# First pairs loaded four tokens to a partition, and attention values multiplied in 64x64 quarters, in a fused attention and feed-forward kernel

## The chip, the cores and the metric

The kernel runs on one core of one Trainium2 chip. A core has a matrix engine (TensorE, PE in the profile, with its weight loads as PEld), VectorE (DVE), ScalarE (ACT) and GpSimd (POOL), which run their own instruction streams and wait for each other by semaphores, and a queue of transfers that SyncE (SP) issues. On-chip memory is SBUF, 128 partitions wide, and PSUM, where TensorE's products land[...]. The metric is device time in microseconds; the time before is the median of three runs.

## The reference

Two blocks follow each other, all in fp32:

```python
# q, k, v: (8, 12, 448, 64)
q_n, k_n = rmsnorm(q, g_q), rmsnorm(k, g_k)          # x / sqrt(mean(x*x) + 1e-6) * g
scores = (1 / sqrt(64)) * q_n @ k_n.transpose(0, 1, 3, 2)
attn = softmax(scores)                                # over the keys
x = (attn @ v) as (8*448, 12*64)                      # 3584 tokens, 768 wide
h = x @ w_in                                          # w_in (768, 1024)
solu = h * softmax(h)
out = layernorm(solu) * g_ln @ w_out                  # w_out (1024, 768)
```

The weights arrive as 64-bit floats, so the kernel converts them itself.

## The kernel before

Only `fast_path` matters here (a general path stands behind a branch for unusual inputs). It has three stages: attention, the product with `w_in` (line 990), the product with `w_out` (line 1205). The last two use a scheme with seven products of sub-blocks instead of eight, and this change doesn't touch them.

Attention runs over 24 *quads* m = 0 to 23. A quad is four heads in two pairs, a = 2m and b = 2m + 1. 448 tokens are three blocks of 128 keys (kc = 0, 1, 2) and a last block of 64. Each fp32 product that the program writes appears as two TensorE instructions in the profile. Per quad:

- `scores(n, kc)` (line 812) makes the scores of one pair and key block: keys on the output's partitions, 448 queries on its columns, in four 64x64 tiles of the array (two halves of the keys by two heads), into a PSUM tile `s` of two banks. `exponentials` (line 802, ScalarE) turns `s` into `E`. `scores_last(m)` (line 825) does the last 64 keys of both pairs. So a quad has seven score units, and seven exponentials.
- `values_last(m)` (line 858) starts the output tiles `o` of both pairs with the last key block, in 64x64 tiles.
- `values(n)` (line 869) adds the three big key blocks of pair n: 128 keys on the array's rows and a head's 64 columns, so two tiles of 128x64, one per head.
- `sums(m)` (line 891) sums `E` over the keys with a matrix of ones, in tiles of 128x32, partly after `add` (line 839, VectorE) and `add_more` (line 848, GpSimd) have added some of the `E` tiles. `inverse` (lines 902 to 910) and `divide` (lines 917, 918) follow on VectorE and GpSimd, and `store_x` (line 926) writes the result to DRAM.

For later quads the same loop body prepares q and k: `squares` (672, ScalarE) and `row_sums` (680, VectorE) for quad m + 2, `fold_sums` (690, 691, GpSimd), `rsqrt_seed` (697, 698, ScalarE) and `rsqrt_step` (704 to 707, VectorE), `normalise` (713, GpSimd), `qk_transpose` (723, VectorE, in 32x32 blocks) and `gain` (727, ScalarE, scales the transposed q) for quad m + 1.

The order is written out by hand (`tc.manual_schedule()`): each engine gets its instructions in the order in which the program names them, and the tile framework adds the semaphore waits that the data require. `unit(f)` names one step of TensorE work and then what is due by `later`. PSUM tiles `s` and the sums tile `sm` share a ring of three buffers (tag "t"), the two `o` tiles another of two.

In twelve quads (`steps_at`: m = 4 to 10, 12, 14, 16, 18, 20) `begin(m)` issues two ScalarE instructions that convert part of `w_in`: line 535, and line 536, which reads what line 535 wrote. `step` issues the VectorE rest (541, 542) a quad later. They stand between the first and the second pair's values in the program.

Pairs 0 and 1 (quad 0) take another way, for a quick start: `load_rows` (line 738) loads tokens to partitions, 112 partitions by four tokens, from SP's and ScalarE's queues; `square_rows` (748, 750), `sum_rows` (756), `normalise_rows` (772, in place), `transpose_rows` (778, TensorE, four transposes of 112 columns into one PSUM tile) and `take_rows` (784 to 788) give the transposed q and k. `gain_column` makes the per-feature gain from `g_q` and `g_k`. Before that, `warm_up` (766) keeps TensorE busy with a product of zeros.

The lines of the loop body that order ScalarE around the values are, before the change:

```python
            if next2:
                squares(a + 4)
                squares(b + 4)
                row_sums(a + 4)
            if next1:
                gain(a + 2)
                gain(b + 2)
            ...
            unit(outputs)        # values_last(m), values(a)
            step(m - 2)
            begin(m)             # lines 535, 536 in twelve quads
            step(m - 1)
            ...
            unit(lambda: values(b))
            unit(lambda: sums(m))
```

Of the kernel before, what the change touches and what calls it, by code (L numbers as in the profile page):

```python
# [9 lines left out]
FP32 = mybir.dt.float32  # L10
U32 = mybir.dt.uint32
I32 = mybir.dt.int32
AX = mybir.AxisListType.X
AF = mybir.ActivationFunctionType
OP = AluOpType
# [351 lines left out]
def fast_path(  # L367
# [24 lines left out]
    nc = tc.nc  # L392
    B, H, S, D = q.shape
    DM, DFF = moe_w_in.shape
    P = 128
# [336 lines left out]
    def load_rows(n, queues):  # L732
        b, hp = divmod(n, NP)
        d = st[n] = {}
        d["qk"] = xs.tile([P, 2, 4, P], FP32, tag="x", name="x")[0:R]
        for s, src in enumerate((q, k)):
            for h in range(2):
                queues[2 * s + h].dma_start(
                    d["qk"][:, s, :, h * D : (h + 1) * D], src[b, 4 * (hp // 2) + hp % 2 + 2 * h].rearrange("(j p) d -> p j d", p=R)
                )  # L740

    def square_rows(n, s, engine):
        d = st[n]
        if s == 0:
            d["sq"] = xs.tile([P, 2, 4, P], FP32, tag="x", name="xsq")[0:R]
        x, y = d["qk"][:, s], d["sq"][:, s]
        if engine is nc.scalar:
            nc.scalar.activation(y, x, AF.Square)
        else:
            engine.tensor_tensor(y, x, x, OP.mult)  # L750

    def sum_rows(n, s):
        d = st[n]
        if s == 0:
            d["ss"] = small.tile([P, 4 * NB], FP32, tag="ss", name="ss", bufs=2)[0:R, 0:16]
        nc.vector.tensor_reduce(
            d["ss"][:, s * 8 : s * 8 + 8], d["sq"][:, s].rearrange("p j (h d) -> p (j h) d", h=2), AX, OP.add
        )

    def warm_up():  # L760
# [4 lines left out]
        for _ in range(5):  # L765
            nc.tensor.matmul(o, w[:, 0:P], w, start=True, stop=True)

    def normalise_rows(n, s):
        d = st[n]
        x = d["qk"][:, s].rearrange("p j (h d) -> p (j h) d", h=2)  # L770
        y = d["y"][:, s * 8 : s * 8 + 8].rearrange("p i -> p i ()").to_broadcast([R, 8, D])
        nc.vector.tensor_tensor(x, x, y, OP.mult)

    def transpose_rows(n, s):
        d = st[n]
        d["pt", s] = ps_t.tile([P, S], FP32, tag="o", name="pt", bufs=2)
        for j in range(4):
            nc.tensor.transpose(d["pt", s][:, j * R : (j + 1) * R], d["qk"][:, s, j], ident[0:R, 0:R])

    def take_rows(n, s):  # L780
        d = st[n]
# [22 lines left out]
    def scores(n, kc):  # L804
        d = st[n]
        s = ps_t.tile([P, 2, 512], FP32, tag="t", name="s")

        for c in range(0, P, D):
            for h in range(2):
                hh = slice(h * D, (h + 1) * D)  # L810
                keys = slice(NJ * c + kc, NJ * (c + D - 1) + kc + 1, NJ)
                nc.tensor.matmul(  # L812
                    s[c : c + D, h, 0:S], d["qkT"][hh, 1, keys], d["qkT"][hh, 0, :],
                    start=True, stop=True,
                )
        exponentials(d, kc, s)
# [19 lines left out]
    def add(n):  # L836
        d = st[n]
        d["es"] = work.tile([P, 2, S], FP32, tag="es", name="es")
        nc.vector.tensor_tensor(d["es"], d["E", 0], d["E", 1], OP.add)  # L839

    def whole(n):
        return on_vector(n // 2) or n % 2 == 0

# [6 lines left out]
    def values_last(m):  # L850

        d = quads[m]
        for i in range(2):
            o = st[2 * m + i]["o"] = ps_t.tile([P, S], FP32, tag="o", name="o", bufs=2)
        for h in range(2):
            for i in range(2):
                pp = slice(i * D, (i + 1) * D)
                nc.tensor.matmul(  # L858
                    st[2 * m + i]["o"][h * D : (h + 1) * D, :], d["vl"][pp, h], d["E", NJ][pp, h],
                    start=True, stop=False,  # L860
                )

    def values(n):


        d = st[n]
        for kc in range(NJ):
            for h in range(2):
                nc.tensor.matmul(  # L869
                    d["o"][h * D : (h + 1) * D, :], quads[n // 2]["v"][:, n % 2 + 2 * h, kc], d["E", kc][:, h],  # L870
                    start=False, stop=(kc == NJ - 1),
                )
# [444 lines left out]
    def unit(f, steps=4):  # L1317
        nonlocal now
        f()
        now += steps  # L1320
        due = [x for x in todo if x[0] <= now]
        todo[:] = [x for x in todo if x[0] > now]
        for _, g in sorted(due, key=lambda x: x[0]):
            g()
# [40 lines left out]
    with tc.manual_schedule():  # L1365
# [19 lines left out]
        for m in range(NQ):  # L1385
            a, b = 2 * m, 2 * m + 1

            def outputs():
                values_last(m)
                values(a)  # L1390


            next1 = m + 1 < NQ
            next2 = m + 2 < NQ
            next3 = m + 3 < NQ
            early = m > 0 and next1

            def norms_next():
                rsqrt_seed(norms[m + 1])
                rsqrt_step(norms[m + 1])  # L1400
                normalise(a + 2)
                normalise(b + 2)

            if m == 0:
                unit(lambda: scores(a, 0))
                normalise_rows(1, 0)
                normalise_rows(1, 1)
                unit(lambda: scores(a, 1))
                unit(lambda: scores(a, 2))
                squares_half(3, 0, True)  # L1410
                for s in range(2):
                    transpose_rows(1, s)
                    take_rows(1, s)
                squares(2)
                squares_half(3, 1, False)
                add(a)
                add_more(a)
                row_sums(2)
                unit(lambda: scores_last(m))
                row_sums(3)  # L1420
                fold_sums(1)
                unit(lambda: scores(b, 0))
                unit(lambda: scores(b, 1))
                add(b)
                norms_next()
                unit(lambda: scores(b, 2))
                squares(4)
                row_sums(4)
                squares(5)
                unit(outputs)  # L1430
                qk_transpose(2)
                gain(2)
                row_sums(5)
                qk_transpose(3)
                fold_sums(2)
                unit(lambda: values(b))
                unit(lambda: sums(m))
                inverse(m)
                later(1, lambda m=m: divide(m))
                continue  # L1440
            if early:
                norms_next()
            for x in joins_at.get(m, ()):
                combine_in(x)
            if next1:
                load_v(m + 1)
            if m == 1:
                load(m + 3)
            unit(lambda: scores(a, 0))
            if m == 1:  # L1450
                gain(3)
            store_x(m - 1)
            if early:
                qk_transpose(a + 2)
                if next3 and m > 1:
                    load(m + 3)
            unit(lambda: scores(a, 1))
            unit(lambda: scores(a, 2))
            unit(lambda: scores_last(m))
            unit(lambda: scores(b, 0))  # L1460
            unit(lambda: scores(b, 1))
            if early:
                qk_transpose(b + 2)
            add(a)
            if not on_vector(m):
                add_more(a)
            unit(lambda: scores(b, 2))
            if next2:
                squares(a + 4)
                squares(b + 4)  # L1470
                row_sums(a + 4)
            if next1:
                gain(a + 2)
                gain(b + 2)
            if next2:
                row_sums(b + 4)
                fold_sums(m + 2)
            add(b)
            if on_vector(m):
                add_more(a)  # L1480
                add_more(b)
            unit(outputs)
            step(m - 2)
            begin(m)
            step(m - 1)
            if m - 1 in sets:
                load_next()
            if m == 2:
                load_next()
                load_next()  # L1490
            if m == 3:
                norm_gain()
            unit(lambda: values(b))
            if m == NQ - 1:
                block_sums(0, 0)
                block_sums(0, 1)
                load_x(1)
            unit(lambda: sums(m))
            inverse(m)
            if next1:  # L1500
                later(1, lambda m=m: divide(m))
            if m == NQ - 2:
                load_x(0)
                sizes(0)
# [188 lines left out]
```

## Time and profile before

| what | value |
|---|---|
| median of three runs (lowest, highest) | 802.53 us (802.07, 803.22) |
| the profiled execution's time | 803.36 us |
| its span, first to last instruction | 801.6 us |
| mean granted TensorE clock | 0.999 |
| first score product starts | 10.58 us |
| attention's last sums end, `w_in` product starts | 316.26 us |
| one quad of attention, from 33 us to 296 us | 12.52 us (12.83 for m = 3) |
| TensorE / VectorE / ScalarE / GpSimd busy | 98% / 77% / 59% / 65% |

A line of the order of time gives start and length in us, the engine, the kernel's line, the operation, output and inputs by the program's names, the tile of the array (rows*columns) for TensorE, the shape and how many instructions were merged into the line. A bracket holds idle time before it and what ended that. TensorE's instructions overlap, so the distance from start to start says more than the lengths. In a line of waits stand the engine and line that waited, what it waited for, the total in us, how often, and the longest. ACTq is the sequencer of ScalarE, which runs semaphore-only instructions.

### The profile page before, as it was taken

The page shows a single profiled execution, that of the slowest core. Times are in us where ns is not written, and L with a number is a line of the kernel's source. Part 1 is how long each engine was busy: PE and PEld are TensorE (multiplying, and loading weights), DVE is VectorE, ACT ScalarE, POOL GpSimd, SP SyncE. Part 2 cuts the span into 40 slices and gives each one's busy share as a digit, 9 for nine tenths or more (in the row PEclk, how much of TensorE's full clock was granted, in tenths as well). Part 3 has the DMA queues.
Part 4 walks back from the last instruction along what each step waited for, and adds up shares of the span by engine and source line. Part 5 has one row for each costly group of instructions (what it writes and reads, how often), then busy time and mean ns, then how long its engine had stood idle before and what let it go on. Part 6 is the DMA issues. An engine that isn't in the chain of part 4 may idle for free.

```text
span 801.6 us, 14271 instructions
## 1 busy us (share of the span) xinstructions
PE 788.1 (98%) x4854; PEld 462.7 (58%) x4854; DVE 613.7 (77%) x1202; ACT 472.2 (59%) x783; POOL 523.1 (65%) x664
## 2 busy tenths in 40 slices
PE   8999999999999999999999999999999999999997
PEld 4344444444444443444444444444789999999996
DVE  6787989989888896488878666777896776866945
ACT  6677878878778774376766544444515455464420
POOL 2666777778876784234456467668698777877861
PEclk9999999999999999999999999999999999999999
DMA  9878889897787832445554435552757457366312
GB/s 169 164 174 156 175 194 186 194 189 161 169 157 169 158 102 75 136 117 155 152 146 131 113 98 141 142 137 52 190 167 233 147 183 264 123 221 223 112 61 83
DMA packets 269598, 122.68 MB, mean 153 GB/s; under 512 B 187596, under 2 KB 254668, under 8 KB 269516
## 3 DMA queue, kind: packets, MB, share of 16 engines
q1 hardware_dynamic: 254332, 111.78, 55.9%
q10 hardware_dynamic: 15184, 9.90, 4.5%
q8 instruction: 40, 0.66, 0.3%
q14 instruction: 42, 0.34, 0.1%
HBM read 84.94 MB, written 36.70 MB: 152 GB/s over the span
## 4 chain that ended last, share of the span: by engine, by line
PE 87%; DVE 3%; DMA 2%; SPq 2%; POOL 2%; ACT 2%; issue 1%; DVEq 0%; ACTq 0%; POOLq 0%
PE A L1205 14%; PE A L990 13%; PE o L869 12%; PE s L812 12%; PE B L990 8%; PE B L1205 7%; PE C L990 4%; PE sm L891 4%; PE D L990 4%; PE C L1205 3%; PE s L825 2%; PE o L858 2%; SPq L636 1%; DMA xg<-xd 1%; ACT E L802 1%
## 5 line engine op out<-in xcount | busy, mean ns | idle before, releaser
L802 ACT ACTIVATE E<-s 128x896 f32<-128x896 f32 x168 | 138.8, 937 | 8.3 <-PE s L812 7.8
L812 PE MATMUL s<-qkT 64*64 64x448 f32 x1152 | 120.1, 545 | 1.0 <-ACT qkT L786 0.6
L869 PE MATMUL o<-E,v 128*64 128x448 f32 x576 | 113.8, 543 | 0.0
L1079 POOL TENSOR_TENSOR he<-he,mhalf 128x1 f32<-128x1 f32 x28 | 27.4, 977 | 102.5 <-DVE he L1078 97.4
L812 PEld LDWEIGHTS s<-qkT 64*64 64x64 f32 x1152 | 48.0, 163 | 59.4 <-ACT E L802 29.3
L1205 PE MATMUL A<-w_out,sums 128*128 128x192 f32 x392 | 79.9, 327 | 1.6 <-POOL sums L1185 1.2
L869 PEld LDWEIGHTS o<-E,v 128*64 128x64 f32 x576 | 39.1, 137 | 72.2 <-issue 68.0
L1205 PE MATMUL B<-w_out,sums 128*128 128x192 f32 x392 | 79.8, 326 | 0.5 <-DVE P L1267 0.5
L713 POOL TENSOR_TENSOR qkn<-qk,ny 128x896 f32<-128x896 f32 x46 | 77.2, 1699 | 3.8 <-DMA qk<-in_q_dram 1.5
L848 POOL TENSOR_TENSOR es<-es,E 128x896 f32<-128x896 f32 x22 | 46.4, 2110 | 48.8 <-ACT sq L672 34.0
L990 PE MATMUL B<-w_in,xsum 128*128 128x512 f32 x168 | 76.7, 592 | 0.0
L990 PE MATMUL A<-w_in,xg 128*128 128x512 f32 x168 | 74.6, 593 | 0.0
L1061 ACT ACTIVATE u<-h,hmax 128x1024 f32<-128x1024 f32 x28 | 32.2, 1148 | 66.8 <-DVE hmax L1055 66.8
L1205 PEld LDWEIGHTS A<-w_out,sums 128*128 128x128 f32 x392 | 66.1, 190 | 2.4 <-POOL sums L1185 1.5
L1205 PEld LDWEIGHTS B<-w_out,sums 128*128 128x128 f32 x392 | 66.2, 190 | 0.8 <-DVE P L1267 0.8
L839 DVE TENSOR_TENSOR es<-E 128x896 f32<-128x896 f32 x48 | 53.9, 1124 | 2.7 <-ACT E L802 2.7
L990 PEld LDWEIGHTS B<-w_in,xsum 128*128 128x128 f32 x168 | 31.9, 190 | 40.2 <-issue 39.2
L990 PEld LDWEIGHTS A<-w_in,xg 128*128 128x128 f32 x168 | 31.8, 190 | 40.1 <-issue 39.3
L690 POOL COPY ss<-part 32x56 f32<-32x56 f32 x92 | 47.0, 511 | 5.9 <-DVE part L680 1.4
L680 DVE TENSOR_REDUCE part<-sq 128x28 f32<-128x896 f32 x46 | 47.9, 1080 | 3.9 <-ACT sq L672 1.6
L723 DVE STREAM_TRANSPOSE qkT<-qkn 128x896 f32<-128x896 f32 x46 | 48.4, 1087 | 0.0
L563 POOL TENSOR_TENSOR w_out<-w_out 128x384 f32<-128x384 f32 x44 | 45.0, 1028 | 1.3
(153 smaller groups left out, 1651.0 us busy)
## 6 DMA issues: line engine op xcount, KB each, us to landing
ur<-ud SPq DMA_DIRECT2D x60, 256.0 KB, 4.6
ud<-ub SPq DMA_DIRECT2D x112, 128.0 KB, 2.3
xd<-xo SPq DMA_DIRECT2D x48, 224.0 KB, 3.0
qk<-in_q_dram SPq DMA_DIRECT2D x92, 112.0 KB, 3.1
qk<-in_k_dram SPq DMA_DIRECT2D x92, 112.0 KB, 3.0
v<-in_v_dram SPq DMA_DIRECT2D x24, 384.0 KB, 4.3
out_dram<-P SPq DMA_DIRECT2D x19, 384.0 KB, 4.2
raw<-in_moe_w_in_dram SPq DMA_DIRECT2D x12, 512.0 KB, 5.3
```

The source lines that it names most:

```text
L563: nc.gpsimd.tensor_tensor(o, p, q, OP.subtract)
L680: nc.vector.tensor_reduce(norms[m]["part"][:, i], st[n]["sq"], AX, OP.add)
L690: e.tensor_copy(ss[g * 32 : g * 32 + 32], part[o * 32 : o * 32 + 32])
L713: e.tensor_tensor(d["qkn"].rearrange("p (s b) d -> p s b d", s=2), d["qk"].rearrange("p s (b d) -> p s b d", d=32), y.rearrange("p (s b) - ...
L723: nc.vector.transpose(d["qkT"].rearrange("p s t -> p (s t)"), d["qkn"].rearrange("p b d -> p (b d)"))
L802: nc.scalar.activation(d["E", kc], s[:, :, 0:S], AF.Exp)
L812: nc.tensor.matmul(s[c : c + D, h, 0:S], d["qkT"][hh, 1, keys], d["qkT"][hh, 0, :], start=True, stop=True,)
L839: nc.vector.tensor_tensor(d["es"], d["E", 0], d["E", 1], OP.add)
L848: e.tensor_tensor(d["es"], d["es"], d["E", 2], OP.add)
L869: nc.tensor.matmul(d["o"][h * D : (h + 1) * D, :], quads[n // 2]["v"][:, n % 2 + 2 * h, kc], d["E", kc][:, h], start=False, stop=(kc == NJ ...
L990: nc.tensor.matmul(k[bank], a[:, c], w_in[i][:, c], start=begin and c == 0, stop=c == HD - 1, skip_group_check=not begin,)
L1205: nc.tensor.matmul(k[bank], a[:, c].rearrange("p a i -> p (a i)"), w_out[:, area, i, c], start=begin and c == 0, stop=c == KC - 1, skip_gr ...
```

## The change

Four things change.

1. First pairs. `load_rows` puts four successive tokens on a partition, (p j) in place of (j p), so that a partition's run in DRAM is 1 KB instead of 256 B. `normalise_rows` writes into the tile of the squares instead of in place, in the order that the transposes want; transpose j writes every fourth column of the PSUM tile, so that tokens come out in order.
2. Values of quads 1 to 22 (`halved`). `values_part(m, part)` replaces `values(a)` and `values(b)`: both pairs at once, in 64x64 tiles, half of each key block's rows a time. In part 0 pair a uses rows 0 to 63 and pair b rows 64 to 127; in part 1 they change over, so each row tile writes into the other pair's PSUM bank.
3. Between the parts stands `turn(m)`: an empty ScalarE instruction that waits for the last product of part 0, and for which the first product of part 1 waits. On ScalarE it is named after `begin(m)`.
4. Order. The score unit (a, 0) of the next quad is named between the two parts, so its exponential comes before the next quad's seeds; a quad m > 1 starts with unit (a, 1). `gain(a + 2)` goes ahead of the squares, `gain(b + 2)` behind `turn`.

VectorE, GpSimd and SP keep the order of their instructions.

```diff
@@ load_rows
-        d["qk"] = xs.tile([P, 2, 4, P], FP32, tag="x", name="x")[0:R]
+        d["qk"] = xs.tile([P, 2, 2, 4, D], FP32, tag="x", name="x")[0:R]
...
-                    d["qk"][:, s, :, h * D : (h + 1) * D], src[b, 4 * (hp // 2) + hp % 2 + 2 * h].rearrange("(j p) d -> p j d", p=R)
+                    d["qk"][:, s, h], src[b, 4 * (hp // 2) + hp % 2 + 2 * h].rearrange("(p j) d -> p j d", p=R)
@@ normalise_rows, transpose_rows
-        x = d["qk"][:, s].rearrange("p j (h d) -> p (j h) d", h=2)
-        y = d["y"][:, s * 8 : s * 8 + 8].rearrange("p i -> p i ()").to_broadcast([R, 8, D])
-        nc.vector.tensor_tensor(x, x, y, OP.mult)
+        y = d["y"][:, s * 8 : s * 8 + 8].rearrange("p (h j) -> p h j ()", h=2).to_broadcast([R, 2, 4, D])
+        o = flat(d["sq"][:, s]).rearrange("p (j h d) -> p h j d", h=2, d=D)
+        nc.vector.tensor_tensor(o, d["qk"][:, s], y, OP.mult)
...
-            nc.tensor.transpose(d["pt", s][:, j * R : (j + 1) * R], d["qk"][:, s, j], ident[0:R, 0:R])
+            nc.tensor.transpose(
+                d["pt", s].rearrange("p (r j) -> p j r", j=4)[:, j], flat(d["sq"][:, s])[:, j * P : (j + 1) * P], ident[0:R, 0:R]
+            )
@@ new
+    def halved(m):
+        return 0 < m < NQ - 1
...
+    def values_part(m, part):
+        first = None
+        for kc in range(NJ):
+            for i in range(2):
+                d = st[2 * m + i]
+                pp = slice((part ^ i) * D, (part ^ i) * D + D)
+                for h in range(2):
+                    x = nc.tensor.matmul(
+                        d["o"][h * D : (h + 1) * D, :], quads[m]["v"][pp, i + 2 * h, kc], d["E", kc][pp, h],
+                        start=False, stop=(part == 1 and kc == NJ - 1),
+                    )
+                    first = first or x
+        if part == 0:
+            quads[m]["half"] = x
+        else:
+            behind(first, quads[m]["turn"])
...
+    def turn(m):
+        x = quads[m]["turn"] = nc.scalar.nop()
+        behind(x, quads[m]["half"])
@@ loop over quads
                 values_last(m)
-                values(a)
+                if halved(m):
+                    values_part(m, 0)
+                else:
+                    values(a)
...
-            unit(lambda: scores(a, 0))
             if m == 1:
+                unit(lambda: scores(a, 0))
                 gain(3)
+            else:
+                unit(lambda: scores(a, 1))
             store_x(m - 1)
...
-            unit(lambda: scores(a, 1))
+            if m == 1:
+                unit(lambda: scores(a, 1))
             unit(lambda: scores(a, 2))
...
             unit(lambda: scores(b, 2))
+            if next1:
+                gain(a + 2)
             if next2:
                 squares(a + 4)
                 squares(b + 4)
                 row_sums(a + 4)
-            if next1:
-                gain(a + 2)
-                gain(b + 2)
...
-            unit(lambda: values(b))
+            if halved(m):
+                turn(m)
+                gain(b + 2)
+                unit(lambda: scores(a + 2, 0))
+                unit(lambda: values_part(m, 1))
+            else:
+                unit(lambda: values(b))
```

More of the change, by code (lines that the diff above doesn't have):

```diff
@@ L744, in square_rows @@
         if s == 0:
-            d["sq"] = xs.tile([P, 2, 4, P], FP32, tag="x", name="xsq")[0:R]
+            d["sq"] = xs.tile([P, 2, 2, 4, D], FP32, tag="x", name="xsq")[0:R]
         x, y = d["qk"][:, s], d["sq"][:, s]
@@ L756, in sum_rows @@
         nc.vector.tensor_reduce(
-            d["ss"][:, s * 8 : s * 8 + 8], d["sq"][:, s].rearrange("p j (h d) -> p (j h) d", h=2), AX, OP.add
+            d["ss"][:, s * 8 : s * 8 + 8], d["sq"][:, s].rearrange("p h j d -> p (h j) d"), AX, OP.add
         )
@@ L766, in warm_up, with flat @@
             nc.tensor.matmul(o, w[:, 0:P], w, start=True, stop=True)
+    def flat(x):
+        return x.rearrange("p h j d -> p (h j d)")
     def normalise_rows(n, s):
         d = st[n]
-        x = d["qk"][:, s].rearrange("p j (h d) -> p (j h) d", h=2)
-        y = d["y"][:, s * 8 : s * 8 + 8].rearrange("p i -> p i ()").to_broadcast([R, 8, D])
-        nc.vector.tensor_tensor(x, x, y, OP.mult)
+        y = d["y"][:, s * 8 : s * 8 + 8].rearrange("p (h j) -> p h j ()", h=2).to_broadcast([R, 2, 4, D])
+        o = flat(d["sq"][:, s]).rearrange("p (j h d) -> p h j d", h=2, d=D)
+        nc.vector.tensor_tensor(o, d["qk"][:, s], y, OP.mult)
     def transpose_rows(n, s):
@@ L861, in values_last, with behind @@
                 )
+    def values_part(m, part):
[14 more added lines that the diff above has]
+            behind(first, quads[m]["turn"])
+    def behind(x, y):
+        tc.add_manual_dep(
+            getattr(x, "ins", x), getattr(y, "ins", y).name,
+            mybir.DependencyInfo(mybir.DependencyClass.Sync, mybir.DependencyReason.DATA),
+            reason="row tiles change banks",
+        )
+    def turn(m):
+        x = quads[m]["turn"] = nc.scalar.nop()
+        behind(x, quads[m]["half"])
     def values(n):
```

## The prediction

> **What bounds the kernel now.** I read the page's head first, then TensorE's order of time over one quad of heads, then ScalarE's over the same quad.
>
> ```profile
> span 801.6 us, 14271 instructions
> PE 788.1 (98%) x4854; PEld 462.7 (58%) x4854; DVE 613.7 (77%) x1202; ACT 472.2 (59%) x783; POOL 523.1 (65%) x664
> PEclk9999999999999999999999999999999999999999
> ```
>
> TensorE is busy for 98% of the span at the full clock, so a microsecond that is added to or taken from its stream counts in full. In attention the stream repeats every 12.52 us (145.55 to 158.07 below; columns: start, length, engine, line, what):
>
> ```profile
> 145.55 0.93 PE L858 MATMUL o<-E,vl 64*64 64x448 f32 x8
> 146.41 4.73 PE L869 MATMUL o<-E,v 128*64 128x448 f32 x24
> 151.07 0.96 PE L891 MATMUL sm<-E,ones 128*32 128x224 f32 x16
> 151.85 0.94 PE L891 MATMUL sm<-es,ones 128*32 128x224 f32 x16
> 152.72 2.52 PE L812 MATMUL s<-qkT 64*64 64x448 f32 x24
> 155.06 0.93 PE L825 MATMUL s<-qkT 64*64 64x448 f32 x8
> 155.81 2.44 PE L812 MATMUL s<-qkT 64*64 64x448 f32 x24
> 158.07 0.93 PE L858 MATMUL o<-E,vl 64*64 64x448 f32 x8
> ```
>
> From start to start, 24 score instructions in 64x64 quarters (four at a time, 6 steps) take 158.07-155.81 = 2.26 us, 0.376 a step. The last-block values (8 instructions, 2 steps, 0.75 us of work) take 0.86: 0.11 is lost where the array goes from 64x64 to 128x64. The main values (24, two at a time, 12 steps, 4.51 us of work) take 4.66. Their first step takes 0.43 (the weight loads stand at 146.41, 146.84, 147.21), 0.05 over; the remaining 0.10 goes at the change to 128x32.
>
> ScalarE in that quad:
>
> ```profile
> 141.29 5.77 ACT L802 ACTIVATE E<-s 128x896 f32<-128x896 f32 x7
> 146.88 1.84 ACT L672 ACTIVATE sq<-qk 128x896 f32<-128x896 f32 x2
> 148.57 1.27 ACT L727 ACTIVATE qkT<-qkT,gcol 128x448 f32<-128x448 f32 x2
> 149.69 0.82 ACT L535 ACTIVATE tmp<-raw,seven 128x512 f32<-128x512 uint32 x1
> 150.54 0.63 ACT L536 ACTIVATE tmp<-tmp 128x512 int32<-128x512 f32 x1
> ```
>
> It has time to spare per quad, but its order matters below. From these starts: an exponential every 0.80 (5.59/7), a square every 0.84, a gain every 0.56, and L536 0.85 after L535. L535 and L536 convert input weights; the pair stands in 12 of the 24 quads (m = 4 to 10, 12, 14, 16, 18, 20), always before TensorE's sums.
>
> **What the Trainium skill says.** "TensorEngine Tiling (Array Packing)", Key Properties: a change of tiling mode drains the array. The 0.11 and 0.10 agree. Same page, Gotcha 1: different row tiles may not use one PSUM bank at the same time and software has to order them; that is why the change has a wait between the two halves of the values. "Perfetto Trace Analysis", DVE / Act Engine Instruction: an instruction is pushed into a wait queue, and then the sequencer is free for the next one. The trace differs, in the only place where it matters here. Two consecutive ScalarE lines, and the semaphore-only instruction that follows them in the program (L1085's, in the first feed-forward product):
>
> ```profile
> 435.74 0.63 ACT L535 ACTIVATE tmp<-raw,seven 128x384 f32<-128x384 uint32 x1
> 436.41 0.52 ACT L536 ACTIVATE tmp<-tmp 128x384 int32<-128x384 f32 x1
> ```
> ```profile
> L1085 ACTq EVENT_SEMAPHORE  x1: 17/17/17, 436.4 to 436.4; - x1
> ```
>
> L536 reads what L535 writes and waits for it. The semaphore instruction behind it ran at 436.415, 6 ns after L536 began at 436.409; at 382.344 and 382.351 it is the same with 7 ns. So it was held until L536's wait was over. It wasn't held behind instructions that only had to execute: on GpSimd such instructions of L713 ran at 153.90, while the first of four copies of L910 ran.
>
> **The change part by part.** I count from the first score product of a quad, in the trace's own durations.
>
> *Mode changes, 22 quads (m = 1 to 22).* Values in quarters need 48 instructions, four at a time: again 12 steps of 0.376. The array no longer leaves 64x64 until the sums. Gain 0.11 + 0.05 = 0.16 a quad. Unseen is the direct change from 64x64 to 128x32: at worst it costs the 0.16 more (no gain), at best nothing (gain 0.26); I take it as dear as today's 0.10. 22 x 0.16 = 3.5 us.
>
> *The wait between the halves.* The second half waits for an empty ScalarE instruction (it becomes a semaphore-only one) that waits for the first half. TensorE now: six score units end at 0.09 + 12 x 0.376 = 4.59 (0.09 is the long first step after the mode change: 155.06-152.72 is 2.34 for 6 steps), last-block values 5.34, first half 7.60, the next quad's first score unit 8.35; there the second half wants to begin. The first half's last products finish about 7.77 (a product lasts 0.54).
>
> *In 10 quads without L535/L536* the empty instruction stands behind exponentials, gain, squares, of which none waits for ScalarE itself. It can pass at about 7.85 (TensorE to VectorE takes 0.07 after the sums), TensorE hears by 7.9 (ScalarE to TensorE 0.05: 154.72 to 154.77), and the score unit hides it until 8.35. If that cover were gone, it would cost about 0.3 a quad. Net -0.16 each: **-1.6 us**.
>
> *In 12 quads with them* it stands behind L536. The first exponential starts at 1.08 (153.80-152.72; its product's end sets this). There are now six before the tail, since the seventh moved behind it: 1.08 + 6 x 0.80 = 5.87; gain(a+2) 6.43; two squares 8.11; L535, and L536 begins at 8.96. Then TensorE hears at about 9.03: 0.68 after 8.35. With the exposed first weight load, the 0.09 again, the stall is 0.77. ScalarE can't be earlier, as its exponentials hang on this quad's scores. Queued behind the waiting product on TensorE: the second half, the sums, then the next scores, so all of it shifts. Net +0.61 each: **+7.3 us**. Bounds: 0.5 (6 us of stall in all) if the first step isn't long and the signals are quicker, 1.0 (12 us) if signals and restart take twice as long.
>
> *Moved steps at no cost.* gain(a+2) ahead of the squares: needs the transpose that ended at 158.36 (5.64), so it can start at 5.87; its reader wants it at 7.6. Squares stay at the same place of the quad (six exponentials and a gain against seven), so sums of squares, the GpSimd fold and the seeds keep their time. gain(b+2) and exponential (a+2,0) follow the wait, done by 9.6 or 11.0, before the seeds at 12.8. GpSimd's round (normalise, transpose, add, fold, seed, step) closes in about 12.46 by its own durations; it binds quads of 12.36 by 0.1 in the first three at most, 0.3 us if no buffer hides it. SP and POOL issue the same transfers in the same order. Last quads: m = 23's first exponential no longer sits behind the size check (TensorE idles 1.0 there), but the check's transfer shifts with the order too; I count -0.1, bounds 0 and -0.8.
>
> *First pairs.* 448 runs of 256 B become 112 of 1 KB in each of eight transfers. The trace's packets take 18 ns for 256 B and 46 ns for 1 KB: with 16 engines 28 x 18 = 0.50 against 7 x 46 = 0.32 us, 0.18 each. The start:
>
> ```profile
> DVE xsq L750 <- DMA x<-in_q_dram: 3.3, 1, 3.3
> ACT xsq L748 <- DMA x<-in_k_dram: 2.9, 1, 2.9
> ```
>
> q's second head lands third of four: 3 x 0.18 = 0.55 earlier, and VectorE's chain from 4.57 to the first scores at 10.58 moves with it; the gains behind them in the queue land earlier also. Bounds: 0.2 (landing set by issue and latency) and 1.0 (all DMA of the first 20 us, 96% busy, gains). Normalising into the square's tile and writing every fourth PSUM column keep element counts; taken as equal, at most 0.1 for 16 small transposes. **-0.55 us**.
>
> *Sum.* -0.55 - 1.6 + 7.3 - 0.1 = **+5.05 us**: a span of 801.6 + 5.05 = 806.7. The profiled execution took 803.36, 1.8 more than its span, and 0.83 more than the median of 802.53; on the median the sum gives **807.6**.
>
> **The rivals.**
> A. The empty instruction isn't held: it passes when the first half ends in all 22 quads. For it: the skill's wait queue, and the GpSimd case. Against: both records at L536. Then -0.55 - 3.5 - 0.1: 798.4. What decides is the stall per converting quad: below 4.15/12 = 0.35 us the change wins, that is, if TensorE hears before 8.35 + 0.35 = 8.70.
> B. Quarters are slower as values than as scores (twice the weight loads, another bank order). At 0.39 a step it is 12 x 0.014 x 22 = 3.7 more: about 811.3. Against: scores keep 0.376 with the same shape.
> C. Stall and gains cancel: a stall near 0.35, time within 0.2% (1.6 us, about what a measurement of this kernel tells from no change): 802.5.
>
> **How the numbers follow.** Main 0.77 (own range 804.5 to 811), A 0.14, B 0.06, C 0.03. The main case's upper bound and B reach 813; the lower end takes the smallest stall with the largest start gain, 803. That leaves out A and a tail. Faster 0.15 (A and a little), same 0.03, slower 0.82.
>
> **What would show it.** Right: quads of about 12.36 where m has no L535 and 13.1 where it has; second halves released by ScalarE's sequencer just after L536 begins; no gap between last-block and main values; first scores near 10.0. Wrong: 12.36 in every quad (A), or steps longer than 0.376 in the values (B).

## The result

The changed kernel takes 808.80 us (median; 808.35 to 809.61), the kernel before 802.58 us (802.07 to 803.22) on the same chip: a ratio of 1.0078 [1.0061, 1.0096]. It is slower by 6.2 us, 0.8%. The profiled executions differ by as much: spans of 807.8 and 801.6 us.

The head of the changed kernel's page, and its group of the values in quarters. The last pair of numbers in a group is the idle time just before it and what ended that:

```profile
span 807.8 us, 15345 instructions
...
PE 790.1 (98%) x5382; PEld 492.8 (61%) x5382; DVE 614.5 (76%) x1202; ACT 472.6 (59%) x783; POOL 523.2 (65%) x664
...
L880 PE MATMUL o<-E,v 64*64 64x448 f32 x1056 | 111.8, 538 | 4.5 <-ACTq L898 4.5
```

There are 528 more products and as many more weight loads (22 quads of 24). TensorE's busy time grew by only 2.0 us; the group line says that the values waited 4.5 us for ScalarE's sequencer at line 898, the empty instruction of `turn`. Such idle time begins where the products before end (each lasts 0.54 us), not where the next one was due, so it understates the loss; the order of time gives the full price. Here is TensorE from the last-block values of a quad with a weight conversion on, and then the same piece of the next quad, which has none:

```profile
148.76 1.05 PE L866 MATMUL o<-E,vl 64*64 64x448 f32 x8
149.51 2.55 PE L880 MATMUL o<-E,v 64*64 64x448 f32 x24
151.76 1.05 PE L817 MATMUL s<-qkT 64*64 64x448 f32 x8
153.19 2.49 PE L880 MATMUL o<-E,v 64*64 64x448 f32 x24 [0.38 <-ACTq L898]
155.61 0.96 PE L929 MATMUL sm<-E,ones 128*32 128x224 f32 x16
156.39 0.94 PE L929 MATMUL sm<-es,ones 128*32 128x224 f32 x16
157.26 1.76 PE L817 MATMUL s<-qkT 64*64 64x448 f32 x16
158.85 0.93 PE L830 MATMUL s<-qkT 64*64 64x448 f32 x8
159.60 2.44 PE L817 MATMUL s<-qkT 64*64 64x448 f32 x24
161.85 1.04 PE L866 MATMUL o<-E,vl 64*64 64x448 f32 x8
162.60 2.54 PE L880 MATMUL o<-E,v 64*64 64x448 f32 x24
164.86 1.04 PE L817 MATMUL s<-qkT 64*64 64x448 f32 x8
165.61 2.54 PE L880 MATMUL o<-E,v 64*64 64x448 f32 x24
168.09 0.96 PE L929 MATMUL sm<-E,ones 128*32 128x224 f32 x16
```

The next quad's score unit (two steps, 0.75 us) starts at 151.76, so the second half was due at 152.51. It begins at 153.19: 0.68 late. In the quad without a conversion it begins at 165.61, 0.75 after 164.86, on time. From 148.76 to 161.85 is 13.09 us; this period was 12.52 before.

ScalarE in the first of these quads, and the records of the empty instruction (count, duration in ns, first and last start), with the line of those who waited for it (us, times):

```profile
150.04 0.71 ACT L727 ACTIVATE qkT<-qkT,gcol 128x448 f32<-128x448 f32 x1
150.60 1.83 ACT L672 ACTIVATE sq<-qk 128x896 f32<-128x896 f32 x2
152.28 0.80 ACT L535 ACTIVATE tmp<-raw,seven 128x512 f32<-128x512 uint32 x1
153.12 0.63 ACT L536 ACTIVATE tmp<-tmp 128x512 int32<-128x512 f32 x1
```
```profile
L898 ACTq EVENT_SEMAPHORE  x22: 17/17/17, 35.4 to 305.5; - x22
...
  PEld o L880: 13.5, 12
```

All 22 ran, and weight loads waited for 12 of them: the twelve quads with conversions. In this quad the empty instruction ran 7 ns after line 536 began at 153.12 (5 to 7 ns in the twelve quads), as the prediction read it from line 1085 before. What line 536 waits for is line 535, which ended 0.03 us before.

Where the span went. A quad is counted from the first score product after one quad's sums to the next such product; a unit of 0.75 us moved from each quad to its predecessor, which matters only in the first and last row:

| part | before, us | after, us | difference |
|---|---|---|---|
| first scores start | 10.58 | 10.17 | -0.41 |
| quad 1 starts | 25.51 | 25.09 | -0.42 |
| quad 1 (0.75 of work pulled in) | 14.25 | 14.84 | -0.16 without it |
| quad 2 | 12.52 | 12.85 | +0.33 |
| quad 3 | 12.82 | 12.83 | +0.01 |
| 12 quads with conversions, each | 12.52 | 13.09 | +0.57, in all +6.85 |
| m = 11, 13, 15, 17, 19, 21, each | 12.52 | 12.48 | -0.04, in all -0.24 |
| quad 22 | 12.27 | 12.25 | -0.02 |
| quad 23 up to the `w_in` product (0.75 done already) | 13.58 | 13.50 | +0.67 without it |
| `w_in` product starts | 316.26 | 323.32 | +7.06 |
| the rest of the span | 485.3 | 484.5 | -0.8 |

The rest has the same instructions, and yet it is 0.8 us shorter. The other traces repeat it: the rest takes 485.3 to 485.4 us in the three kernels with the old order of attention (the kernel before and two of the experiments below) and 484.5 to 484.9 in the five with the new one. Its cause is open.

### The profile page after: what moved, and what is told of

The parts are those of the page before. It is cut to its first block, busy times and chain, and to the rows that moved or that the text cites. A ratio compares the mean times of both kernels' runs of the same rounds, so it can differ in the third digit from the quotient of the medians.

```text
span 807.8 us, 15345 instructions
## 1 busy us (share of the span) xinstructions
PE 790.1 (98%) x5382; PEld 492.8 (61%) x5382; DVE 614.5 (76%) x1202; ACT 472.6 (59%) x783; POOL 523.2 (65%) x664
## 4 chain that ended last, share of the span: by engine, by line
PE 72%; ACT 10%; DVE 6%; SPq 3%; DMA 3%; POOL 3%; issue 2%; ACTq 0%; DVEq 0%; POOLq 0%
PE A L1243 14%; PE A L1028 13%; PE B L1028 8%; PE o L880 7%; PE B L1243 7%; PE s L817 5%; ACT E L807 5%; PE C L1028 4%; PE D L1028 4%; PE sm L929 4%; PE C L1243 3%; ACT sq L672 2%; SPq L636 2%; DMA xg<-xd 1%; ACT tmp L535 1%
## 5 line engine op out<-in xcount | busy, mean ns | idle before, releaser
L807 ACT ACTIVATE E<-s 128x896 f32<-128x896 f32 x168 | 141.0, 931 | 16.0 <-PE s L817 15.9
L817 PE MATMUL s<-qkT 64*64 64x448 f32 x1152 | 126.9, 545 | 2.8 <-ACT E L807 1.7
L880 PE MATMUL o<-E,v 64*64 64x448 f32 x1056 | 111.8, 538 | 4.5 <-ACTq L898 4.5
L817 PEld LDWEIGHTS s<-qkT 64*64 64x64 f32 x1152 | 54.2, 163 | 55.7 <-ACT E L807 27.5
L880 PEld LDWEIGHTS o<-E,v 64*64 64x64 f32 x1056 | 57.7, 133 | 48.0 <-issue 15.7
L844 DVE TENSOR_TENSOR es<-E 128x896 f32<-128x896 f32 x48 | 56.7, 1182 | 2.7 <-ACT E L807 2.7
L1243 PE MATMUL A<-w_out,s 128*128 128x192 f32 x224 | 45.6, 326 | 0.0
```

Source lines behind the costliest of these rows:

```text
L807: nc.scalar.activation(d["E", kc], s[:, :, 0:S], AF.Exp)
L817: nc.tensor.matmul(s[c : c + D, h, 0:S], d["qkT"][hh, 1, keys], d["qkT"][hh, 0, :], start=True, stop=True,)
L880: x = nc.tensor.matmul(d["o"][h * D : (h + 1) * D, :], quads[m]["v"][pp, i + 2 * h, kc], d["E", kc][pp, h], start=False, stop=(part == 1 a ...
L1243: nc.tensor.matmul(k[bank], a[:, c].rearrange("p a i -> p (a i)"), w_out[:, area, i, c], start=begin and c == 0, stop=c == KC - 1, skip_gr ...
```

## The experiments

**The empty instruction ahead of the conversion.** One line is moved: `turn(m)` is named right after the quad's values instead of behind `begin(m)`.

```diff
             unit(outputs)
+            if halved(m):
+                turn(m)
             step(m - 2)
             begin(m)
...
             if halved(m):
-                turn(m)
                 gain(b + 2)
```

> The whole change, with the empty instruction named before the conversion pair (lines 535, 536) instead of behind it. Theory (it is held until line 536's wait for line 535 is over): the twelve converting quads fall from 13.09 to the 12.48 of the plain ones, 12 x 0.61 = 7.3 us less than the change, about 801.5. Rival (the stall has another cause, such as the row tiles' change of banks itself): converting quads stay near 13.1 and the time at 808.8.

It took 801.76 us (801.14 to 802.98), 0.9985 [0.9976, 0.9993] of the kernel before, which took 803.03 in this comparison. The stall is gone in all twelve quads. TensorE in one of them:

```profile
157.81 1.05 PE L866 MATMUL o<-E,vl 64*64 64x448 f32 x8
158.56 2.55 PE L880 MATMUL o<-E,v 64*64 64x448 f32 x24
160.81 1.05 PE L817 MATMUL s<-qkT 64*64 64x448 f32 x8
161.57 2.55 PE L880 MATMUL o<-E,v 64*64 64x448 f32 x24
164.05 0.96 PE L929 MATMUL sm<-E,ones 128*32 128x224 f32 x16
...
170.29 1.04 PE L866 MATMUL o<-E,vl 64*64 64x448 f32 x8
```

The second half follows after 0.76, and the quad takes 12.48 (157.81 to 170.29). So the place of one ScalarE instruction is worth 7.0 us by the medians (808.80 - 801.76) and 7.5 by the two ratios to the kernel before (1.0078 and 0.9985); twelve times 13.09 - 12.48 is 7.3. The stall is more than the whole loss. But with the stall gone the kernel gains only 1.2 us on the kernel before, by the ratio, not the 4 of the prediction's rival A. A quad stays at 12.48 where the prediction had 12.36.

**The empty instruction between the two conversion instructions.** This separates two readings of "held": is it enough that work stands ahead of it on ScalarE, or must the work ahead itself be waiting? The main part of the edit (in quads without a conversion the empty instruction stays where the change has it):

```diff
             nc.scalar.activation(low, lo, AF.Relu, scale=-(2.0 ** -29), bias=seven)   # line 535
+            if between:
+                between.pop()()       # turn(m)
             nc.scalar.activation(tmp[:, 1].bitcast(I32), low, AF.Copy, scale=-1.0, bias=7.0)   # line 536
```

> The whole change, with the empty instruction between the two conversion instructions. Theory (only an instruction that itself waits holds it; line 535 has nothing to wait for): it passes when the first half ends, before line 535 is done, and converting quads take 12.48; about 801.5. Rival (it is held until ScalarE has executed all that is ahead of it, so line 535 as well): it passes at the same moment as in the change, converting quads take 13.09, about 808.8.

One execution, the profiled one: 803.27 us with a span of 801.5 (the profiled execution of the first experiment took 802.98), and quads of 12.49. In this kernel the lines are 902 for the empty instruction, 537 and 540 for the two conversions; the record of a converting quad and ScalarE's order of time:

```profile
L902 ACTq EVENT_SEMAPHORE  x1: 17/17/17, 148.6 to 148.6; - x1
```
```profile
147.04 1.83 ACT L676 ACTIVATE sq<-qk 128x896 f32<-128x896 f32 x2
148.72 0.81 ACT L537 ACTIVATE tmp<-raw,seven 128x512 f32<-128x512 uint32 x1
149.56 0.63 ACT L540 ACTIVATE tmp<-tmp 128x512 int32<-128x512 f32 x1
```

It ran at 148.57, while the squares were still running and 0.15 us before line 537 began, although line 537 stands ahead of it in the program. So an instruction that is only waiting its turn doesn't hold it; the one whose wait on a semaphore is still open (the second conversion, for the first) does. The number of instructions ahead is not what decides: here line 537 stood ahead and had not begun, and in the changed kernel line 536 likewise, while line 535 ran. Nor need the wait be for ScalarE itself. In the kernel before, nine exponentials between 25 and 290 us waited for TensorE, 0.36 to 1.18 us each, and each time ScalarE's next semaphore instruction ran 5 to 7 ns after the exponential began.

**One transpose a division.** The four 64x64 tiles of the array can run apart: in the changed kernel's plain quad above, the last-block values last 1.04 instead of 0.93, and each line after them too is 0.1 longer. In the trace's single products, one of the four of a step starts first and the other three 0.11 us after it (162.61 and 162.72 in the first step of line 880). What the second pair's values wait for shows best in quad 2, where the wait is longest. TensorE's weight loads and VectorE's instruction of the division, in the changed kernel:

```profile
44.15 0.13 PEld L866 LDWEIGHTS o<-E,vl 64*64 64x64 f32 x1 [0.19 <-issue]
44.52 0.13 PEld L866 LDWEIGHTS o<-E,vl 64*64 64x64 f32 x1 [0.24 <-issue]
44.96 0.14 PEld L866 LDWEIGHTS o<-E,vl 64*64 64x64 f32 x3 [0.30 <-DVE xo L956]
```
```profile
44.28 0.62 DVE L956 TENSOR_TENSOR xo<-o,r 128x448 f32<-128x448 f32 x1
```

Pair b's output tile is free when the division of the previous quad's pair b (line 956, ending 44.90) has read it. One tile goes on alone (the first two weight loads) and three wait. The program names the products of the last block head by head, pair a before pair b, so pair a's second head stands behind pair b's first. In later quads it is the same by a hair: the first tile's weight load starts at 161.48, line 956 ends at 161.86, and the loads of the three others start at 161.92. To test it, the division is made shorter: the two transposes of reciprocals (0.65 us each) become one of twice the size, on top of the first experiment.

```diff
+        r = work.tile([P, 2 * NB, 32], FP32, tag="r", name="r", bufs=1)
+        nc.vector.transpose(r, quads[m]["rc"].rearrange("p i t b -> p (i t b) ()").to_broadcast([P, 2 * NB, 32]))
...
-            r = work.tile([P, NB, 32], FP32, tag="r", name="r", bufs=1)
-            nc.vector.transpose(r, quads[m]["rc"][:, i].rearrange("p t b -> p (t b) ()").to_broadcast([P, NB, 32]))
-            nc.vector.tensor_tensor(xo[:, i], st[n]["o"], r.rearrange("d b i -> d (b i)"), OP.mult)
+            nc.vector.tensor_tensor(xo[:, i], st[n]["o"], r[:, i * NB : (i + 1) * NB].rearrange("d b i -> d (b i)"), OP.mult)
```

> As the kernel with the empty instruction first, and the two transposes of the division (two of 448 columns, about 0.67 us each from start to start) as one of 896, so that the second division ends some 0.2 us earlier. Theory (plain quads lost 0.11 of their gain because the last-block values of pair b wait for that division, and its row tile then lags until the sums): quads go from 12.48 to about 12.38, 22 x 0.1 = 2.2 us less, about 799.3. Rival (going from 64x64 straight to 128x32 costs 0.23 by itself): quads stay at 12.48, about 801.5.

It took 799.04 us (798.45 to 800.01), 0.9951 of the kernel before [0.9935, 0.9968]. It beats both kernels. TensorE in the quad that the first experiment showed:

```profile
156.48 0.93 PE L866 MATMUL o<-E,vl 64*64 64x448 f32 x8
157.23 2.43 PE L880 MATMUL o<-E,v 64*64 64x448 f32 x24
159.49 0.93 PE L817 MATMUL s<-qkT 64*64 64x448 f32 x8
160.24 2.44 PE L880 MATMUL o<-E,v 64*64 64x448 f32 x24
162.60 0.96 PE L929 MATMUL sm<-E,ones 128*32 128x224 f32 x16
...
168.85 0.93 PE L866 MATMUL o<-E,vl 64*64 64x448 f32 x8
```

The lengths are 0.93 and 2.44 again: no lag. The second half and the change to the sums take 162.60 - 160.24 = 2.36; with the lag it was 164.05 - 161.57 = 2.48. The quad is 12.37, what the prediction had for its mode changes alone, and quad 2 went from 12.85 to 12.52.

**The same transpose in the kernel before.** A control: does a shorter division help by itself?

> The kernel before with one part alone: the two transposes of a division (448 columns each) made one of 896 columns. Theory (the single transpose helps the changed kernel only because there the last block's values start 0.75 us sooner after the sums and reach the division; in the kernel before they start later and the division is hidden): quads stay 12.52 us, the time 802.2 to 803.2. Rival (the single transpose shortens the division's loop or VectorE's load in any kernel): quads 12.37 us, the time about 799.5.

802.71 us (801.83 to 804.26), a ratio of 0.9995 [0.9987, 1.0004]; the quads stay at 12.52. There the last-block values began a score unit later, and the division was hidden, as two lines of the kernel before show:

```profile
156.72 0.62 DVE L918 TENSOR_TENSOR xo<-o,r 128x448 f32<-128x448 f32 x1
157.69 0.15 PEld L858 LDWEIGHTS o<-E,vl 64*64 64x64 f32 x4 [0.20 <-issue]
```

The division ends at 157.34, 0.35 us before all four tiles load their weights. Moving these loads 0.75 us closer uses that up: it is the new order that put the division on the path.

**The first pairs alone.** The kernel before with only the new load, normalisation and transposes of quad 0.

> The kernel before with only the new way of loading, normalising and transposing the first pairs. Theory: first scores at 10.18 instead of 10.58 and all of attention 0.4 us earlier, about 802.2. Rival (the gain is lost again behind the transfers for quads 1 and 2): first scores at 10.18 but quad 1 at 25.5 as before, 802.6.

802.13 us (801.69 to 803.77), 0.9990 [0.9981, 0.9999]: a gain at the edge of what can be told, 0.1 to 1.5 us. In its trace the first scores start at 10.08 (10.58 before), and quad 1 at 25.01 (25.51): 0.5 us earlier. The direction holds over the traces, the size doesn't: in the six with the new way of loading quad 1 starts between 25.01 and 25.33, in the two with the old one at 25.51 and 25.87. The `w_in` product starts at 316.54 all the same, since quad 23 took 14.37 there, for the reason that follows.

**The sizes of rows out of the way.** At the end of attention ScalarE waits for a transfer before it takes row sums for the size check, and six exponentials stand behind it. The changed kernel, ScalarE and TensorE in quad 23:

```profile
311.32 0.84 ACT L989 ACTIVATE xsum<-xg 128x768 f32<-128x768 f32 x1 [4.13 <-DMA xg<-xd]
...
313.13 4.93 ACT L807 ACTIVATE E<-s 128x896 f32<-128x896 f32 x6
...
314.08 2.63 PE L817 MATMUL s<-qkT 64*64 64x448 f32 x24 [1.74 <-ACT E L807]
```

The transfer was issued at 303.49 and its data used 7.8 us later. In the kernel before that took 7.1 (296.34 to 303.45), and in five other kernels 7.8 to 8.4, among them the control with the single transpose (7.9), which has the order of the kernel before. Quad 23 took 13.58 us before, but 14.37 and 14.04 in the two experiments with the old order, against 14.25 (with the moved unit) in the changed kernel. So the 0.7 us that this comparison of two profiled executions puts on quad 23 is most likely the quick landing in the one profile of before; one profile a kernel doesn't settle it. I then moved the row sums behind the last scores, on top of the fastest kernel:

```diff
+            if m == NQ - 1:
+                sizes(0)          # behind scores_last(m), instead of at the end of quad 22
```

> The kernel with the turn put first and one transpose a division, and in it the sizes of the next two images' rows moved from the end of the last quad but one to behind the last scores of the last step, so that the eight exponentials of the last pair stand ahead of the row sums' wait on ScalarE. Theory (in the last two steps TensorE waits for exponentials that are held behind the row transfer of the sizes: 1.74 us in the profile of the changed kernel): the wait goes, the last step up to the w_in product is 1.0 to 1.7 us shorter, the time about 797.6. Rival (the wait moves on: the sizes themselves, or what the w_in stage needs of them, then end last): about 799.0, with the wait shown at or behind the w_in product.

799.59 us (799.09 to 800.22), 0.9962 [0.9948, 0.9976] of the kernel before: no gain on the 0.9951 without this edit (measured on another chip). The wait moved on, as the rival had it. VectorE and TensorE at the end of attention:

```profile
308.43 3.69 DVE L856 TENSOR_TENSOR es<-es,E 128x896 f32<-128x896 f32 x2
```
```profile
310.09 0.59 PE L929 MATMUL sm<-E,ones 128*32 128x224 f32 x8
310.49 0.56 PE L929 MATMUL sm<-es,ones 128*32 128x224 f32 x8
312.17 0.59 PE L929 MATMUL sm<-es,ones 128*32 128x224 f32 x8 [1.12 <-DVE es L856]
```

The scores no longer wait, but the sums now do, for the additions on VectorE (308.43 to 312.12); in the kernel without this edit these ended at 312.27. The `w_in` product starts 0.86 us earlier in this trace (312.69 against 313.55), less than the 1.0 to 1.7 expected, and the medians don't show it.

## Why the prediction was right, and where not

The direction, the cause and the size held: 807.6 was predicted, with 804.5 to 811 as the main case's own range, and 808.8 measured. The signs on which it relied are there: second halves released by ScalarE's sequencer just after line 536 begins, in twelve quads and no others. Term by term, in the span up to the `w_in` product:

| term | predicted, us | measured, us |
|---|---|---|
| start, up to quad 1 | -0.55 | -0.42 |
| 10 quads without conversions | -1.6 | -0.08 |
| 12 quads with conversions | +7.3 | +6.85 |
| last quads | -0.1 | +0.67 |
| sum | +5.05 | +7.0 |

- **The wait in converting quads.** Predicted stall 0.77, of which 0.68 for being late and 0.09 for a long first step. The lateness is 0.68. The first step cost less: from 153.19 to 155.61 is 2.42, only 0.06 over the 2.36 without a wait. A net of +0.57 against +0.61: right. No run here leaves the wait between the halves out, so whether the row tiles need it is not shown.
- **Rival A.** Refuted: the instruction was held. With it out of the way rival A's time (798.4) still didn't come, for the reason of the next point.
- **The mode changes.** Price right, net wrong. The array gives 0.15 a quad when nothing else is late (12.37 in the kernel with one transpose), against 0.16, and the unseen change from 64x64 to 128x32 costs the 0.10 assumed (2.36 for six steps of 0.376). But in the changed kernel the six plain quads from m = 11 gained 0.04 each, and quad 2 lost 0.33. The step that failed is "moved steps at no cost": moving the score unit (a, 0) ahead of the sums brings the last-block values 0.75 us closer to them, and I didn't name what they wait for, the division that frees their output tile. It ended up to 0.3 us too late. The wait held three of the four tiles. "TensorEngine Tiling (Array Packing)", Key Properties, states that tiles operate independently; this trace agrees, and adds what it costs: their 0.11 us lag runs through all four groups of products unseen and is paid once, at the change to the 128x32 tiles of the sums, which span all 128 rows.
- **Rival B.** Refuted: in the kernel with one transpose, twelve steps of values take 12 x 0.376 = 4.51 plus the 0.10 of the change.
- **First pairs.** VectorE's wait for q's load went from 3.3 to 2.8 us, the changed kernel's line being

```profile
DVE xsq L750 <- DMA x<-in_q_dram: 2.8, 1, 2.8
```

  so 0.5 of the predicted 0.55, of which 0.4 reached the first scores in this pair of traces. Alone, the edit brings 0.8 us by the ratio of times (0.1 to 1.5) and 0.5 by the trace at quad 1.
- **Last quads.** Sign wrong in the comparison of traces (+0.67); the landing time of one transfer varies over the kernels from 7.1 to 8.4 us, by far more than the term. I took it as fixed.

The terms missed by +1.5 (plain quads), -0.45, +0.13 and +0.77, and the part behind attention, which it took as unchanged, by -0.8; that the total is off by only 1.2 us is partly chance.

## What to carry to other kernels

When work is moved forward on the bottleneck engine, list for each moved instruction what it waits for and when that ends now, the release of its output buffer included: a cover of a few tenths is used up without any line of the diff naming it. A semaphore-only instruction on ScalarE was free here where nothing ahead of it still waited on a semaphore, and cost 0.6 us a quad behind one that did; so look at the waits ahead of it, and name it ahead of a dependent pair where the data allow. And where tiles of the array run apart, as here, a lag shows first as longer lines in the order of time, and its price came only at the change to tiles that span all rows.

## What the runs showed that I had not expected

- An empty ScalarE instruction overtakes, in time, an engine instruction that stands ahead of it: it ran 0.15 us before line 537 began. It did not pass one whose own semaphore wait was open: it ran 5 to 7 ns after line 536's start, in all twelve quads.
- One VectorE transpose of 896 columns takes 1.11 us, against two of 448 columns at 0.65 us each. That 0.19 us in the right place was worth 2.7 us (801.76 to 799.04).
- The attention rows, written to DRAM and read back, took between 7.1 and 8.4 us from the read's issue to the first use in seven like kernels, enough to hide a gain of half a microsecond.
